# Attention and Fourier mixing on one core: the last head pairs of the first query half go to the output projection through DRAM, two pairs to one set of products

## The chip, the core and the metric

The kernel runs on one core of a Trainium2 chip. Its engines work side by side and wait for each other by semaphores: PE (TensorE, matrix products; its weight loads are listed apart as PEld), ACT (ScalarE), DVE (VectorE), POOL (GpSimd) and SP (SyncE, which here only issues DMAs). Each engine works through its own instructions in the order of the program. A DMA can be issued from SP, from ACT or from POOL, each with a queue of its own; the same 16 DMA engines carry them. The metric is the device time of one execution in microseconds (us); lower is better.

## The reference

Two branches over one input x (2048 rows, 512 columns), mixed by a gate per row:

```python
qkv = (x @ wqkv).reshape(B, S, 3, H, Dh)          # H = 32 heads of Dh = 16
p = softmax(q @ k.T * Dh ** -0.5)                 # per head, 2048 x 2048
a = concat_heads(p @ v) @ wo                      # the output projection
b = dft_seq_re @ (x @ dft_hid_re.T) - dft_seq_im @ (x @ dft_hid_im.T)
g = sigmoid((x * gate_w).sum(-1))
out = g * a + (1 - g) * b
```

Operands of the large products are held as a rounded part and a rest ("hi" and "lo", names ending in h and l); a product is then three: hi·hi, hi·lo, lo·hi.

## The kernel before, in words

The projections, the scans for the softmax's row maxima and most of the Fourier branch come first. The rest is one hand-written loop of 512 steps (line 991), 32 for each of the 16 pairs of heads (16 per half of the queries, h = 0 and 1, of 1024 queries). In a step the scores of one block of 128 keys against 1024 queries go through PE (qk, line 210) and their exponentials through ACT (lines 234 and 242); the products with the values (pv, line 755) are collected in the PSUM bank pvb and run two steps' worth at a time, at even steps. Beside that, each step from 301 on takes one piece of other PE work from the generator `outputs` (`next(fill)`): in an even step before the scores, in an odd step after them, so that two pieces stand together on PE. The pieces are: the last ten row blocks of the Fourier sum (`spectral`, steps 301 to 460), then the output projection: `mix_heads` (pairs 0 to 11), `mix_some` for t = 8, 9, 10, and `mix_some` for t = 0, 1, 2 in steps 505 to 510. The order in which an engine issues its work is the order of the program's text.

**How a pair comes to the projection.** When a pair's half of the queries is summed, `quotients` copies pvb to ob (line 764) and moves the sums of the exponentials into lc by POOL DMAs (767). Some steps later (10; 7 for pair 14; 3 for pair 15) `divide` takes reciprocals (773), spreads them over rb through DRAM (774, 776), multiplies (777) and splits into oh and ol (784, 785). In ob a pair occupies four groups of 32 rows, one for each quarter of the half's queries (c) and each head (j), with 16 rows of values in each: half of the rows carry nothing. Pairs 0 to 13 are written to the DRAM tensors o_d by two POOL DMAs (790). From there they come back without the empty rows: `output_rows` (835) for pairs 0 to 11, four pairs in 128 rows, and `output_rest` (843) for pairs 12 and 13, as 64 rows for each c. Pair 14 (both halves) and pair 15's first half stay in SBUF as they are, rows with gaps; pair 15's second half goes by another way after the loop.

**The products for pairs 12 to 15.** `direct[h]` is the list of their operands for a half, `w4` the list of the rows of wo that belong to them, both of three: k = 0 for pairs 12 and 13 together, k = 1 for pair 14, k = 2 for pair 15. `mix_rest(t, ps, k)` is three products of two matmuls each, one matmul for the row block t and one for t + 4, on 64 rows of the array each. `mix_some(t, parts)` runs k = 0 in one step, all others in the next, and takes the sums into the result on DVE (853); it has parts (0, 1, 2) for t = 0, 1, 2, whose rows are then stored (926), and (0, 1) for t = 8, 9, 10. Block t = 3 and the rest of the second half are finished after the loop by `part`, with `part(3, 0)` in the last step, `part(3, 1)` and `part(3, 2)` placed between the steps of the last pair's division (lines 1051 to 1065).

`output_operands` loads wo's rows for w4 (lines 808 to 816): for k = 0 64 rows twice; for k = 1 and 2 it clears a tile on DVE (810) and loads four groups of 16 rows (812), gaps between.

The lines that the change touches have these numbers: 778 to 788 (where oh and ol are put, and who is not written to DRAM), 809 to 812, 844, 938, 954, 968, 1037 and 1056.

Of the kernel before, what the change touches and what calls it, by code (L numbers as in the profile page):

```python
# [10 lines left out]
F32 = mybir.dt.float32  # L11
F32R = mybir.dt.float32r
# [6 lines left out]
P = 128  # L19
# [3 lines left out]
DH = 16  # L23
NP = H // 2
NB = S // P
ND = D // P
# [27 lines left out]
def build(tc, xT, wqkv, wo, wrT, wiT, cr, ci, gate, out):  # L54
    nc = tc.nc
    with ExitStack() as ctx:
# [130 lines left out]
        def block(i):  # L187
            return big.tile([P, 512], F32R, tag=f"b{i}", name=f"b{i}")
# [541 lines left out]
        with ExitStack() as pa:  # L730
# [40 lines left out]
            def divide(p, h, ob, lc):  # L771

                nc.vector.reciprocal(lc, lc)  # L773
                nc.gpsimd.dma_start(r_d[p][h].rearrange("n (s e) -> (n s) e", e=16), lc)  # L774
                for n, (c, j, r) in enumerate(quads):
                    nc.gpsimd.dma_start(rb[r:r + DH, :], r_d[p][h][n:n + 1, :].to_broadcast([DH, 512]))
                nc.gpsimd.tensor_mul(ob, ob, rb)
                kept = p >= NP - 2
                if p == NP - 2:
                    oh, ol = block(28 + 2 * h), block(29 + 2 * h)  # L780
                else:
                    pool, *tags = (cw, "chi", "clo") if kept else (ap, "oh", "ol")
                    oh, ol = (pool.tile([P, 512], F32R, tag=tag, name=tag) for tag in tags)
                nc.gpsimd.tensor_copy(oh, ob)
                nc.gpsimd.tensor_sub(ol, ob, oh.bitcast(F32))
                if kept:
                    direct.setdefault(h, []).append((oh, ol))
                    return
                for i, s in enumerate((oh, ol)):
                    nc.gpsimd.dma_start(o_d[p // 4][i][h, :, p % 4], s.bitcast(F32))  # L790

# [7 lines left out]
            def output_operands():  # L799

                for n in range(2 * ND - 2):
                    b = [block(6 + 2 * n + i) for i in range(2)]
                    raw = (ap.tile([P, D], F32, tag="craw", name="wor", bufs=2) if n == ND - 2 else
                           ap.tile([P, D], F32, tag="take", name="wor", bufs=3))
                    if n < ND - 1:
                        nc.sync.dma_start(raw, wo[n * P:n * P + P, :].rearrange("(h e) m -> e h m", e=DH))
                    else:
                        base = D - (8, 4, 2)[n - ND + 1] * DH
                        if n >= ND:
                            nc.vector.memset(raw, 0.0)  # L810
                            for c, j, r in quads:
                                nc.sync.dma_start(raw[r:r + DH, :], wo[base + DH * j:base + DH * j + DH, :])
                        else:
                            for r in (0, 64):
                                nc.sync.dma_start(raw[r:r + 64, :],
                                                  wo[base:base + 64, :].rearrange("(h e) m -> e h m", e=DH))
                    raws_.append((raw, b))
                    if n % (ND - 1) == ND - 2:
                        yield
                        yield  # L820
                        for raw, b in raws_:
                            yield
                            nc.vector.tensor_copy(b[0], raw)
                            nc.vector.tensor_sub(b[1], raw, b[0].bitcast(F32))
                            (w2 if n < ND - 1 else w4).append(b)
                        raws_.clear()
                        yield
# [9 lines left out]
            def output_rest(h):  # L837

                a = [block(24 + 2 * h + i) for i in range(2)]
                for i in range(2):  # L840
                    for c in range(2):
                        src = o_d[ND - 1][i][h, c, 0:2].rearrange("p (j r) s -> r (p j) s", j=2)
                        nc.sync.dma_start(a[i][64 * c:64 * c + 64, :].bitcast(F32), src[0:DH])
                direct[h].insert(0, a)

            def load_y(c):
                y4 = stk.tile([P, 4, D], F32, tag="stk", name="y4")
# [80 lines left out]
            def mix_some(t, parts):  # L928

                ps = pair_banks()  # L930
                ps = ps[:, 0, :], ps[:, 1, :]
                for k in parts:
                    mix_rest(t, ps, k, k == parts[0], k == parts[-1])
                    if k == parts[0]:
                        yield
                for j in range(2):
                    take_in(t + 4 * j, ps[j])
                if parts[-1] == 2:
                    store_out(t)
                yield  # L940

            def outputs():

                for t in range(NB - LATER, NB):
                    yield from spectral(t)
                for c in range(NC):
                    for t in range(4 * c, 4 * c + 4):
                        yield from mix_heads(t, (2, 2, 2, 3) if t < 2 * SLOW and t % 2 == 0 else (4, 5))
                    if c < 2:
                        output_rows(c + 2)  # L950
                for t in (8, 9, 10):
                    yield from mix_some(t, (0, 1))
                for t in range(3):
                    yield from mix_some(t, (0, 1, 2))
                yield

            groups = {}
# [1 line left out]
            def part(t, *ks):  # L959

                if t not in groups:
                    if t in (3, 9):
                        ps = pair_banks()
                        groups[t] = ps[:, 0, :], ps[:, 1, :]
                    else:
                        groups[t] = bank2() if t == 8 else (bank(), pvb if t == 11 else bank())
                for k in ks:
                    mix_rest(t, groups[t], k, k == 0 or 7 < t < 11, k == 2)

            now = [0]  # L970
            fill, operands = outputs(), output_operands()
# [19 lines left out]
            for step in range(NP * PERIODS):  # L991
                p, i = step // PERIODS, step % PERIODS
                h, kb = i // NB, i % NB
                now[0] = step
                if i == 18:
                    load_use(p + 1)
                if step in (MIX - 24, MIX - 20):
                    load_unit()
                if step == MIX - 12:
                    split_unit()  # L1000
                if OUT - 10 <= step < OUT - 4 or step >= OUT + 4:
                    next(operands, None)
                if step in (OUT - 12, OUT + 1):
                    output_rows(int(step > OUT))
                if step in (OUT - 25, (NP - 1) * PERIODS):
                    for c in range(2):
                        load_y(c + 2 * (step > OUT))
                if step >= MIX and step % 2 == 0:
                    next(fill)
                if step == 0:  # L1010
                    pend.append((p, h, kb, ahead[:2]))
                    continue
                es = ahead[2:] if step == 1 else [qk2(p, h, kb, 0)]
                if step == 1:
                    es.append(qk2(p, h, kb, 1))
                    flush()
                if late:
                    late.pop(0)()
                if step == 2:
                    es.append(qk2(p, h, kb, 1))  # L1020
                if step > 1:
                    next_scan()
                if step > 2:
                    es.append(qk2(p, h, kb, 1))
                if step >= MIX and step % 2:
                    next(fill)
                if step == NP * PERIODS - 1:
                    part(3, 0)
                done = None
                for _ in range(min(len(pend), 1) if step < MIX else 0 if step % 2 else 2):  # L1030
                    done = flush()
                if done and done[2] == NB - 1:
                    halved.append((step + (10 if done[0] < NP - 2 else 7 if done[0] < NP - 1 else 3), quotients(*done[:2])))
                if halved and halved[0][0] <= step:
                    p_, h_ = halved[0][1][:2]
                    divide(*halved.pop(0)[1])
                    if p_ == NP - 2:
                        output_rest(h_)
                pend.append((p, h, kb, es))
            flush()  # L1040
            flush()
# [11 lines left out]
            turned, spread = bank(), bank()  # L1053
            for q in blocks_:
                nc.tensor.transpose(turned[:, q], ob[:, q], ident)
            part(3, 2)
            rl = sm.tile([P, 16], F32, tag="lc", name="lc")
            nc.vector.reciprocal(rl.rearrange("p (s n) -> p s n", n=4),
                                 turned.rearrange("p (s n m) -> p s n m", n=4, m=32)[:, :, :, DH])
# [56 lines left out]
```

## Time and profile before

| | |
|---|---|
| time, median of 3 runs | 1726.92 us (1726.63 to 1727.53) |
| span of the profiled execution | 1725.2 us |
| what lies around the span (median less span) | 1.7 us |
| instructions | 36082 |
| PE busy | 1713.5 us (99%) |
| ACT, DVE, POOL busy | 1506.8, 1089.1, 648.7 us |
| HBM read, written | 129.63 MB, 61.61 MB |

The span is the time from the first to the last instruction of one execution that the hardware profiler recorded; the profile gives no other time for that execution. Times in the profile's rows are microseconds from the start of the span unless marked ns. L185 is line 185 of the kernel; where a helper issues an operation, the line is the helper's (185 is `halves_of`, which issues all matmuls of `spectral`, `mix_heads` and `mix_rest`). "xy<-b,c" is an operation that writes tile xy from tiles b and c. A row in square brackets ends with the idle time of the engine before it and what ended it. Some records of matmuls can be missing, so a count in a row can be a little low.

### The profile page before, as it was taken

How to read it: one execution, taken by the hardware profiler on the slowest of the kernel's cores; microseconds unless marked ns; L12 is line 12 of the kernel's file. 1: busy time of each engine (PE TensorE's matmuls, PEld its weight loads, DVE VectorE, ACT ScalarE, POOL GpSimd, SP SyncE). 2: the span in 40 equal slices, each digit the busy share in tenths (PEclk: the TensorE clock that was granted, in tenths of full speed). 3: DMA queues.
4: the chain of work that ended last, by engine and by line, in shares of the span. 5: the costliest groups of instructions: out<-in, count | busy, mean ns of one | idle time of the engine just before them, and what ended most of it. 6: DMA issues, size and time to landing. Idle time of an engine off the chain costs nothing.

```text
span 1725.2 us, 36082 instructions
## 1 busy us (share of the span) xinstructions
PE 1713.5 (99%) x13680; PEld 1044.7 (61%) x13680; DVE 1089.1 (63%) x2059; ACT 1506.8 (87%) x2489; POOL 648.7 (38%) x770
## 2 busy tenths in 40 slices
PE   9999999999999999999999999999999999999998
PEld 7888888988888885333333333333455555555554
DVE  6898888999999996666666666666512212122333
ACT  6447889888888888999999999999988888888886
POOL 3672436655555762223233242322322322223222
PEclk9999999999999999999999999999999999999999
DMA  7783557534337663243323342351334244265712
GB/s 257 241 285 75 156 158 211 158 112 115 103 111 211 153 136 72 37 73 58 66 59 67 54 82 44 58 107 37 65 80 94 72 110 91 67 150 139 175 36 101
DMA packets 123710, 193.03 MB, mean 112 GB/s; under 512 B 54112, under 2 KB 56656, under 8 KB 116624
## 3 DMA queue, kind: packets, MB, share of 16 engines
q1 hardware_dynamic: 84464, 170.20, 37.7%
q0 software_dynamic: 38496, 19.47, 5.7%
q8 instruction: 107, 1.75, 0.4%
q10 hardware_dynamic: 576, 1.05, 0.2%
q14 instruction: 67, 0.55, 0.1%
HBM read 129.63 MB, written 61.61 MB: 111 GB/s over the span
## 4 chain that ended last, share of the span: by engine, by line
PE 96%; DVE 2%; DMA 1%; issue 1%; ACT 0%; SPq 0%; DVEq 0%; POOL 0%; ACTq 0%; POOLq 0%
PE pvb L755 29%; PE xy L185 25%; PE s L210 19%; PE s L185 9%; PE s L154 9%; PE s L135 5%; DVE fold L160 1%; DMA q_d<-eh 0%; DMA raws<-wqkv 0%; DMA ks<-kf_d 0%; PE s L554 0%; DVE y L853 0%; ACT fold L158 0%; DVE s L278 0%; DVE b L334 0%
## 5 line engine op out<-in xcount | busy, mean ns | idle before, releaser
L234 ACT ACTIVATE eb<-s 128x1024 f32<-128x1024 f32 x512 | 578.7, 1130 | 65.4 <-PE s L210 65.4
L242 ACT ACTIVATE e<-s 128x512 f32<-128x512 f32 x1022 | 608.9, 709 | 0.4 <-PE s L210 0.4
L137 DVE TENSOR_REDUCE mx<-s 128x2 f32<-128x1024 f32 x364 | 441.4, 1224 | 188.7 <-PE s L135 188.5
L755 PE MATMUL pvb<-eb,va 128*17 128x512 f32 x2052 | 513.0, 597 | 0.0
L755 PE MATMUL pvb<-e,va 128*17 128x512 f32 x2044 | 512.1, 597 | 0.0
L160 DVE CUSTOM_DVE_ANT_0 fold<-s,fold 128x512 f32<-128x512 f32 x660 | 443.9, 690 | 52.7 <-PE s L154 24.4
L158 ACT ACTIVATE fold<-s 128x512 f32<-128x512 f32 x660 | 389.9, 603 | 73.3 <-PE s L154 52.3
L210 PEld LDWEIGHTS s<-qs,ks 50*128 50x128 f32 x2048 | 214.9, 184 | 355.2 <-ACT eb L234 255.1
L210 PE MATMUL s<-qs,ks 50*128 50x512 f32 x2048 | 420.0, 434 | 0.0
L185 PE MATMUL xy<-b,c 64*128 64x512 f32 x2448 | 397.3, 392 | 0.3 <-ACT c L333 0.3
L154 PE MATMUL s<-ks,qs 48*128 48x512 f32 x1320 | 315.3, 405 | 1.6 <-DVE mx L160 1.0
L185 PEld LDWEIGHTS xy<-b,c 64*128 64x128 f32 x2448 | 283.9, 187 | 17.6 <-issue 1.0
L154 PEld LDWEIGHTS s<-ks,qs 48*128 48x128 f32 x1320 | 172.9, 184 | 47.0 <-DVE mx L160 12.5
L774 POOL DMA_DIRECT2D r_d<-lc x31 | 18.1, 583 | 456.4 <-DVE lc L773 456.4
L755 PEld LDWEIGHTS pvb<-eb,va 128*17 128x17 f32 x2052 | 70.5, 96 | 189.9 <-issue 182.7
L135 PE MATMUL s<-ks,qs 48*128 48x512 f32 x728 | 151.6, 394 | 0.7 <-DVE mx L137 0.7
L767 POOL DMA_DIRECT2D lc<-ob x124 | 62.9, 514 | 156.3 <-DVE ob L764 156.1
L185 PE MATMUL xy<-w,b 64*128 64x512 f32 x768 | 115.3, 392 | 0.0
L365 POOL TENSOR_TENSOR c<-craw,c 128x512 fp32r<-128x512 f32 x84 | 109.4, 1302 | 6.7
L185 PE MATMUL s<-b,chi 64*128 64x512 f32 x670 | 105.4, 391 | 0.0
L364 POOL CAST c<-craw 128x512 fp32r<-128x512 f32 x84 | 53.3, 635 | 125.1 <-PE xy L185 120.1
L871 DVE CAST chi<-craw 128x512 fp32r<-128x512 f32 x40 | 19.1, 477 | 111.4 <-PE s L185 99.3
(136 smaller groups left out, 1535.2 us busy)
## 6 DMA issues: line engine op xcount, KB each, us to landing
qs<-q_d SPq DMA_DIRECT2D x66, 256.0 KB
craw<-ci SPq DMA_DIRECT2D x64, 256.0 KB
craw<-cr SPq DMA_DIRECT2D x60, 256.0 KB
ks<-k_d SPq DMA_DIRECT2D x44, 256.0 KB
qs<-q_d SPq DMA_DIRECT2D x66, 128.0 KB
ab_d<-ab SPq DMA_DIRECT2D x32, 256.0 KB
y_d<-y SPq DMA_DIRECT2D x32, 256.0 KB
o_d<-oh POOLq DMA_DIRECT2D x28, 256.0 KB, 13.8
```

Source lines behind the costliest of these rows:

```text
L135: nc.tensor.matmul(ps[:, j, :], qs[b:b + 48, qb * P:(qb + 1) * P], ks[b:b + 48, c * 512:(c + 1) * 512], start=True, stop=True)
L137: nc.vector.tensor_reduce(mx[p][:, :, qb, c], ps, axis=AX.X, op=ALU.max)
L154: nc.tensor.matmul(ps, qs[b:b + 48, qb * P:(qb + 1) * P], ks[b:b + 48, c * 512:(c + 1) * 512], start=True, stop=True)
L158: nc.scalar.activation(fold[j], ps, AF.Relu)
L160: nc.vector.tensor_tensor_reduce(out=fold[j], in0=ps, in1=fold[j], scale=1.0, scalar=-3.0e38, op0=ALU.add, op1=ALU.max, accum_out=mx[p][:, ...
L185: nc.tensor.matmul(ps[j], lhs[r], rhs[r], start=first, stop=last)
L210: nc.tensor.matmul(pss[j], ks[b:b + 50, kb * P:(kb + 1) * P], qs[b:b + 50, q0:q0 + 512], start=True, stop=True)
L234: nc.scalar.activation(e, ps, AF.Exp, scale=SCALE)
L242: nc.scalar.activation(e[j], pss[j], AF.Exp, scale=SCALE)
L365: sub(lo, raw, hi.bitcast(F32))
L755: nc.tensor.matmul(pvb[r:r + VC, :], va[:, kb, 2 * p + j, :], es[c][j], start=kb == 0, stop=kb == NB - 1, tile_position=(0, r))
L767: nc.gpsimd.dma_start(lc[32 * n:32 * n + 32, :], ob[r + DH:r + VC, :].rearrange("p (s e) -> p s e", e=16))
```

## The change

`divide` writes pair 14 (both halves) and the first half of pair 15 to DRAM like the pairs before them. A new function `output_last(h)` reads them back without gaps: for h = 0 pairs 14 and 15, 64 rows for each c; for h = 1 pair 14 alone, 32 rows for each c, with the other 32 cleared on DVE. `output_last(1)` is called with the division of pair 14's second half, `output_last(0)` with the division of pair 15's first half. The weights for k = 1 become the 64 rows of wo for pairs 14 and 15 together, so in the first half of the queries `mix_rest(t, ps, 1)` covers both pairs and k = 2 is left out there. In the second half k = 2 is still pair 15, with gaps.

```diff
                 nc.gpsimd.tensor_mul(ob, ob, rb)
-                kept = p >= NP - 2
-                if p == NP - 2:
-                    oh, ol = block(28 + 2 * h), block(29 + 2 * h)
-                else:
-                    pool, *tags = (cw, "chi", "clo") if kept else (ap, "oh", "ol")
-                    oh, ol = (pool.tile([P, 512], F32R, tag=tag, name=tag) for tag in tags)
+                oh, ol = (ap.tile([P, 512], F32R, tag=tag, name=tag) for tag in ("oh", "ol"))
                 nc.gpsimd.tensor_copy(oh, ob)
                 nc.gpsimd.tensor_sub(ol, ob, oh.bitcast(F32))
-                if kept:
-                    direct.setdefault(h, []).append((oh, ol))
-                    return
                 for i, s in enumerate((oh, ol)):
                     nc.gpsimd.dma_start(o_d[p // 4][i][h, :, p % 4], s.bitcast(F32))
...
-                        if n >= ND:
+                        if n == ND:
+                            for r in (0, 64):
+                                nc.sync.dma_start(raw[r:r + 64, :], wo[base:base + 64, :])
+                        elif n > ND:
                             nc.vector.memset(raw, 0.0)
...
-                direct[h].insert(0, a)
+                direct[h] = [a]
+
+            def output_last(h):
+
+                a, n = [block(28 + 2 * h + i) for i in range(2)], 2 - h
+                for i in range(2):
+                    for c in range(2):
+                        src = o_d[ND - 1][i][h, c, 2:2 + n].rearrange("p (j r) s -> (p j) r s", j=2)
+                        nc.sync.dma_start(a[i][64 * c:64 * c + 32 * n, :].bitcast(F32), src[:, 0:DH])
+                        if n == 1:
+                            nc.vector.memset(a[i][64 * c + 32:64 * c + 64, :].bitcast(F32), 0.0)
+                direct[h].append(a)
...
-                if parts[-1] == 2:
+                if t < NB // 4:
                     store_out(t)
...
-                    yield from mix_some(t, (0, 1, 2))
+                    yield from mix_some(t, (0, 1))
...
-                    mix_rest(t, groups[t], k, k == 0 or 7 < t < 11, k == 2)
+                    mix_rest(t, groups[t], k, k == 0 or 7 < t < 11, k == (2 if t > 3 else 1))
...
                     if p_ == NP - 2:
                         output_rest(h_)
+                    if p_ == NP - 2 + (h_ == 0):
+                        output_last(h_)
...
-            part(3, 2)
```

## The prediction

> **What bounds the kernel now.** I read the page's busy times first, then its chain of work that ended last, then the same chain in order of time for the last 75 us, where all of the change's products stand.
>
> ```profile
> PE 1713.5 (99%) x13680; PEld 1044.7 (61%) x13680; DVE 1089.1 (63%) x2059; ACT 1506.8 (87%) x2489; POOL 648.7 (38%) x770
> ...
> PE 96%; DVE 2%; DMA 1%; issue 1%; ACT 0%; SPq 0%; DVEq 0%; POOL 0%; ACTq 0%; POOLq 0%
> ```
>
> ```profile
> 1679.43 1.41 PE s L185 x11
> ...
> 1683.79 1.38 PE s L185 x12
> ...
> 1688.17 1.41 PE s L185 x12
> ...
> 1692.55 2.09 PE s L185 x16
> 1694.64 0.47 PE s L210 x4
> 1695.11 1.84 PE pvb L755 x16
> 1696.95 0.67 PE s L210 x4
> 1697.62 2.10 PE s L185 x18
> ...
> 1702.69 2.10 PE s L185 x17
> ...
> 1710.65 0.89 PE s L185 x6
> ```
>
> The columns are start, duration and what the chain did. PE holds the chain nearly throughout, so here PE work that goes is time that goes. Two steps make one round: a group of projection products (L185), scores (L210), values (L755), scores. The groups at 1679.43, 1683.79 and 1688.17 are t = 8, 9, 10 with 12 matmuls, those at 1692.55, 1697.62 and 1702.69 are t = 0, 1, 2 with 18 (16 and 17 where records are missing). A round with 12 takes 1688.17 - 1683.79 = 4.38 us, one with 18 takes 1697.62 - 1692.55 = 5.07. So six matmuls cost 0.69 us, or 0.23 for a product of two, and nothing else takes their place as the bound when they are absent: the rounds of 12 already run in this very loop.
>
> **What is removed from PE.** Six matmuls in each of three rounds: 3 x 0.69 = 2.07 us, and `part(3, 2)` behind the loop.
>
> ```profile
> 1712.06 0.73 PE L185 MATMUL s<-b,chi 64*128 64x512 f32 x4
> 1712.63 0.40 PE L185 MATMUL s<-b,clo 64*128 64x512 f32 x2
> ...
> 1713.00 0.53 PEld L1065 LDWEIGHTS s<-ident,rb 128*128 128x128 f32 x4 [0.41 <-DVE rb L1062]
> ...
> 1712.52 0.76 DVE L1062 TENSOR_TENSOR rb<-s,lc 128x256 f32<-128x256 f32 x2
> ```
>
> That group fills PE from 1712.06 to 1713.03. The transposes behind it (L1065) start at 1713.00 and are put down to DVE's product rb, whose first half of two starts at 1712.52 and so ends near 1712.9. Without the group PE stands idle there instead: gain 0 (at most 0.1 us). ACT's scaling of block 3 can come a little earlier, but what ends last runs through the products of t = 8 to 11 behind these transposes. So the gain is 2.07 us, if the operands are there.
>
> **What is added: a trip through DRAM, and whether it is in time.** There are three trips. The critical one is pair 15's first half, whose division ends last.
>
> ```profile
> 1685.73 0.61 POOL L784 CAST chi<-ob 128x512 fp32r<-128x512 f32 x1
> 1686.42 1.27 POOL L785 TENSOR_TENSOR clo<-ob,chi 128x512 fp32r<-128x512 f32 x1
> ...
> 1585.89 1.28 POOL L785 TENSOR_TENSOR ol<-ob,oh 128x512 fp32r<-128x512 f32 x1
> 1587.12 0.88 POOL L790 DMA_DIRECT2D o_d<-oh  x1
> 1587.99 0.82 POOL L790 DMA_DIRECT2D o_d<-ol  x1
> ```
>
> ```profile
> o_d<-oh POOLq DMA_DIRECT2D x28, 256.0 KB, 13.8
> o_d<-ol POOLq DMA_DIRECT2D x28, 256.0 KB, 13.9
> rb<-r_d POOLq DMA_DIRECT2D x124, 32.0 KB, 2.0
> ```
>
> ```profile
> DMA to landing us min/median/max: 9.4/9.8/10.1
> ...
> DMA to landing us min/median/max: 9.1/13.9/20.2
> ```
>
> In the run before, both parts are ready in SBUF at 1686.42 + 1.27 = 1687.69, five us ahead of their use. After the change the two stores follow: pair 13's, in the rows of 1585 to 1588, start 1.23 and 2.10 us after the subtraction's start, so here at 1687.65 and 1688.52. How long they take is the decisive term. Over all 56 stores of this line, issue to landing took 9.1 to 20.2 us, median 13.9. The first of the two landing rows is a pair of stores issued at 818 us while no other bulk transfer ran: 9.4 for oh, 10.1 for ol. From 1687 on the DMA engines are idle too (one instruction fetch of 16 KB in the nine us from 1686 on):
>
> ```profile
> q8 instruction: 1, 0.02, 0.7%
> ...
> L843 SPq DMA_DIRECT2D b<-o_d x8: 514/545/1276, 1613.4 to 1640.2; - x8
> ```
>
> So I take the quiet pair, which is the nearest row: oh lands at 1697.05, ol at 1698.6. SP waits for each and then issues two loads of 128 KB, 0.55 us each (the 514/545/1276 row, ns). A quiet transfer of 32 KB takes 2.0 us to land; the second load, issued 0.6 later, is then there 2.6 us after the store (bounds 2 and 4). So the hi operand is ready at 1699.65, the lo operand at 1701.2.
>
> Needed: t = 0's k = 1, at the head of step 506, comes 0.69 us after the group's start, at 1692.55 + 0.69 = 1693.24. Nothing before that point is shortened. PE waits there, and behind it in PE's own order stand the scores of step 506, so ACT, which has only finished step 505's exponentials, waits too, then the values, then DVE. Nothing covers this: about 6.4 us idle until the hi products (four matmuls, 0.46 us), again until 1701.2, and the last product ends at 1701.45. Before, the whole group of 18 ended at 1694.64: **+6.8 us** at this place. The other two rounds then give 2 x 0.69 = 1.39 back: +5.4.
>
> **The clock after the stall.** The granted TensorE clock is 1.00 in all of the loop. After the last matmul, at 1718.1, it stays and then falls:
>
> ```profile
> 1718.00:1721.00 3.00, 0.07 (x2) 0.00 (x0) 2.16 (x4) 0.02 (x1) 2.03 (x2) 1.00 1.03 379
> 1721.00:1724.00 3.00, 0.00 (x0) 0.00 (x0) 0.00 (x0) 0.00 (x0) 0.00 (x0) 0.52 0.86 319
> ...
> 2.30:3.30 1.00, 1.00 (x6) 1.00 (x5) 1.00 0.96 238
> ...
> 4.30:5.30 1.00, 0.85 (x8) 0.61 (x6) 1.00 0.87 303
> ```
>
> The first two rows (the sixth value behind the colon-separated stretch and its length is the clock) show that some 3 us of idle PE are enough: 0.52 in the stretch from 1721. An idle of 6.4 us is longer than that. How long it then stays at half is bounded by the program's start: there the warm-up transposes go from 6 per us to 8 per us within 3 to 4 us of work. PE-bound work at half clock loses half of that time; part of it falls into the wait for lo. I take **+1.5 us**, bounds 0 (no fall) and 3.4.
>
> The Trainium skill (TensorE: Matmul & The Clock Gate, Part 1: The HAM clock gate) says the clock is halved after an idle window of about 3.4 us and comes back after about 3.4 us of sustained work, with windows that run free of the program. The trace agrees for the fall (about 3 us); by the rule alone the loss would be an estimated 1.7 us.
>
> **The other trips are in time.** Pair 14's second half:
>
> ```profile
> 1655.69 1.29 POOL L785 TENSOR_TENSOR b<-ob,b 128x512 fp32r<-128x512 f32 x1
> ...
> 1647.53 0.24 DVE L773 RECIPROCAL lc<-lc 128x16 f32<-128x16 f32 x1
> 1651.15 1.54 DVE L853 SCALAR_TENSOR_TENSOR y<-s,g,y 128x512 f32<-128x512 f32 x2 [3.38 <-PE s L185]
> 1596.25 1.03 DVE L810 MEMSET wor<- 128x512 f32 x2
> ```
>
> Stores at 1656.9 and 1657.8, landed by 1668, loaded by 1671; needed at 1679.43 + 0.69 = 1680.1. Even the slowest landing (20.2) brings it to 1680.6. Its first half is divided 33 us earlier and needed only with pair 15's. The four clears of 32 rows cost at most 0.52 each (half of the 1.03 row), 2.1 us of DVE right behind the reciprocal of 1647.53, in an idle stretch of 3.38: cost 0; if they had no cover, 2.1. One clear and two of eight small loads of wo go, on DVE and SP beside a bound PE: 0. On SP, only the stores of finished rows stand behind `output_last`, and they come after the products anyway. On POOL nothing stands behind the last two stores before 1713. The tiles oh and ol, now used by three more divisions, are read out (1668) long before the next one writes them (1685.73).
>
> **Sum.** +6.8 - 1.39 + 1.5 + 0 = +6.9 on the span: 1725.2 + 6.9 = 1732.1. The runs' median lies 1.7 over the span: **1733.8 us**.
>
> **Rivals.**
> *The store is quick, no stall.* SP's stores of finished rows are of the same size:
>
> ```profile
> 1705.61 0.99 SPq L926 DMA_DIRECT2D out_dram<-y  x2
> ...
> GB/s 0 0 0 0 0 0 0 0 0 0 0 0 191 328 410 300 355 410 382 382 382 410 383 328 382 437 355 410 410 355 301 82 0 0 0 0 0 0 0 0
> ```
>
> Two of 256 KB, the first issued at 1705.61, and the traffic (slices of 0.075 us from 1705.5) is over at 1707.9: 2.3 us. At that rate ol is in DRAM at 1690.9 and loaded at 1693.5, just before lo's turn at 1693.24 + 0.46; the change then gives its 2.07 us whole: 1724.85, not slower. It decides if both parts are back by 1693.7. Against it: no store of this line landed in under 9.1 us, quiet or not. 5%.
> The Trainium skill (DMA: Bandwidth & Descriptors, Anatomy of one DMA — SWDGE) has about 2.0 us plus the bytes at 436 GB/s for a DMA issued from GpSimd, an estimated 2.6 us for these 256 KB; by that the stall would all but vanish. The rows of this very store (9.4 where quiet) do not agree.
>
> *Stall, but the clock holds* (two short idles instead of one): 1733.8 - 1.5 = 1732.3. For it: the hi products break the idle. 12%.
>
> *The store takes its median*, 13.9 instead of 10.1: +3.8, 1737.6. For it: half of all stores did; against it, those ran beside other traffic, these do not. 10%.
>
> *SP is held earlier.* If `output_rest(0)` had to wait for pair 14's store (same DRAM tensor, other rows; stored from about 1623), the loads behind it on SP, `output_rows(2)` and the rows of y for the second half, would come at 1642 to 1648 rather than by 1640, where t = 8 needs them near 1639: about +5 more, 1739. Against it: SP loads the next rows of y_d 0.38 us after the start of a store to others of its rows, without waiting:
>
> ```profile
> 1550.92 0.33 SPq L893 DMA_DIRECT2D y_d<-y  x1
> 1551.30 0.44 SPq L879 DMA_DIRECT2D y<-y_d  x1
> ```
>
> 3%.
>
> **Chances and range.** The forecast has 70%. Its own bounds: a store 2 us quicker than the quiet pair and no clock loss gives 1730.3, a store 2 us slower and 3 us of loss 1737.3. With the median store inside, the range is 1730.8 to 1738.5; outside it are the quick store, the held SP and tails. A difference of 0.2% (3.45 us) is about what a measurement of this kernel tells from none; even the quick store would gain only 2.07, so it counts as the same. Faster 0.02, same 0.07 (with the lower tail), slower 0.91.
>
> **What would show it.** In the changed kernel's trace: a first group of t = 0 cut in two with an idle PE of some 6 us ended by the DMA from o_d; two stores near 1687.7 with 9 to 10 us to landing; a clock under 1.00 in the us after it; rounds of 4.38 for t = 1 and 2 once the clock is back; no new wait around 1639 or 1680. The prediction is wrong if the stores land within 5 us, or if PE's idle ends by anything else than that load.

## The result: slower, and by nearly twice what was forecast

| | before | after |
|---|---|---|
| time, median | 1727.03 us (1726.63 to 1727.53, 5 runs) | 1739.8 us (1739.1 to 1741.2, 5 runs) |
| ratio to before, 95% interval | | 1.0076 [1.0065, 1.0087] |
| span of the profiled execution | 1725.2 us | 1737.3 us (its own time: 1739.1) |

The forecast was 1733.8 with a range to 1738.5. The spans differ by 12.1 us where 6.9 were forecast, the medians by 12.8.

The busy times and the chain of waits by engine, on the page of the changed kernel:

```profile
PE 1714.9 (99%) x13656; PEld 1037.3 (60%) x13656; DVE 1088.6 (63%) x2062; ACT 1506.7 (87%) x2489; POOL 653.5 (38%) x776
...
PE 94%; DMA 2%; DVE 1%; issue 1%; ACT 0%; POOL 0%; SPq 0%; DVEq 0%; POOLq 0%; ACTq 0%
```

24 matmuls are gone, as intended (13680 to 13656), yet PE's busy time grew by 1.4 us, and 2% of the chain, which was 1% before, are now DMAs. The matmuls of line 185 in order of time, in the timeline of the changed kernel's PE (start, duration, what, and in brackets the idle time before it with what ended it):

```profile
1687.93 1.57 PE L185 MATMUL s<-b,b 64*128 64x512 f32 x12
1692.31 0.87 PE L185 MATMUL s<-b,b 64*128 64x512 f32 x6
1701.12 0.79 PE L185 MATMUL s<-b,b 64*128 64x512 f32 x1 [7.94 <-DMA b<-o_d]
1702.40 1.22 PE L185 MATMUL s<-b,b 64*128 64x512 f32 x3 [0.49 <-DMA b<-o_d]
1704.01 0.79 PE L185 MATMUL s<-b,b 64*128 64x512 f32 x1 [0.40 <-DMA b<-o_d]
1705.30 0.79 PE L185 MATMUL s<-b,b 64*128 64x512 f32 x1 [0.49 <-DMA b<-o_d]
1710.61 1.55 PE L185 MATMUL s<-b,b 64*128 64x512 f32 x12
1714.99 1.54 PE L185 MATMUL s<-b,b 64*128 64x512 f32 x12
```

Up to t = 0's k = 0 at 1692.31 nothing has moved (1692.39 before). Then come four waits for the operands from DRAM, one for each of the four loads, and each matmul after a wait takes 0.79 us where 0.39 is usual: the clock. The groups of t = 1 and 2 stand 4.38 us apart, as forecast. The chain in order of time shows of what the waits are made (start, duration, what the chain did):

```profile
1686.43 1.27 POOL ol L780
...
1688.52 11.43 DMA o_d<-ol
...
1699.97 0.51 SPq L847
...
1700.53 4.72 DMA b<-o_d
...
1705.30 0.79 PE s L185
1706.09 0.85 PE s L210 x3
1706.95 3.16 PE pvb L755 x16
...
1712.16 0.49 PE s L210 x4
1712.64 1.84 PE pvb L755 x16
```

The store of ol takes 11.43 us, its two loads from the first issue to the last matmul's start 1705.30 - 1699.97 = 5.3. (The chain follows the load that was issued last; by e4 below the wait would have been about as long with a quicker store of ol.) Behind them the scores and values take 0.85 + 3.16 where the next round takes 0.49 + 1.84. The last projection matmul of t = 0 ends at 1706.09; before, it ended at 1694.64. The granted clock by stretches of 4 us (behind each stretch stand its length, the busy time of PE, PEld, DVE, ACT and POOL, then the clock, the share of the DMA engines and GB/s):

```profile
1692.00:1696.00 4.00, 1.18 (x10) 0.60 (x8) 0.00 (x0) 2.00 (x3) 0.00 (x0) 0.99 0.23 66
1696.00:1700.00 4.00, 0.00 (x0) 0.00 (x0) 0.00 (x0) 0.00 (x0) 0.00 (x0) 0.50 0.15 52
1700.00:1704.00 4.00, 2.01 (x4) 0.78 (x4) 0.00 (x0) 0.00 (x0) 0.00 (x0) 0.50 0.25 94
1704.00:1708.00 4.00, 3.49 (x14) 1.44 (x18) 1.41 (x2) 1.44 (x3) 0.00 (x0) 0.50 0.10 38
1708.00:1712.00 4.00, 4.00 (x29) 1.80 (x23) 0.00 (x0) 1.98 (x5) 0.00 (x0) 0.80 0.29 109
```

It is at half from 1696, some 3 us after the last matmul, until after 1708. The mean of 0.80 in the last stretch means half speed up to about 1709.6, some 4 us after dense work set in at 1705.30. The single matmuls between the four waits had not brought it back: from 1700 to 1704 PE was busy for 2.01 of 4 us, at 0.50.

The Trainium skill (TensorE: Matmul & The Clock Gate, Part 1: The HAM clock gate) asks for about 3.4 us of sustained work, in windows that run free of the program, before the clock returns; the 4 us here agree with that.

**What the loads look like.** During the loads of four heads the 16 DMA engines are about a quarter busy, and the rate is steady. In the DMA view of the changed kernel, 40 slices of a stretch from 1700 to 1704 us, loads of four heads, and one from 1667 to 1674, `output_last(1)` with its loads of two heads:

```profile
GB/s 102 123 102 82 102 123 102 82 102 102 123 82 102 102 102 61 82 62 61 102 102 41 61 41 102 102 82 102 123 102 82 102 123 82 102 82 143 82 82 102
...
GB/s 0 0 35 0 0 0 35 35 47 70 47 47 47 47 59 59 47 47 47 47 59 59 47 23 47 70 47 47 47 47 59 59 47 47 47 35 0 0 0 0
DMA packets 136, 0.26 MB, mean 37 GB/s; under 512 B 8, under 2 KB 8, under 8 KB 136
```

Four heads: about 94 GB/s. Two heads: 47, half of it. The four loads of the second stretch have 8 packets under 512 B beside their 128 rows, two for each load. So the rate goes with the count of the outermost dimension in the transfer's access pattern, some 23.5 GB/s for each of it. `output_rest` reads the same kind of rows with the 16 rows of a head outermost; `output_last` has the heads outermost. That became theory A.

The Trainium skill (DMA: Bandwidth & Descriptors, Why a DMA increments its semaphore by 16 and not by 1) says that a transfer runs on the largest number of DMA engines up to 16 that divides the outermost dimension of both its sides, and that each of them ends with a write to the semaphore. The rates of 94 and 47 and the two small packets for each load of two heads agree with 4 and 2 engines.

### The profile page after: what moved, and what is told of

It is laid out like the page before. It is cut to its first block, busy times and chain, and to the rows that moved or that the text cites. A ratio compares the mean times of both kernels' runs of the same rounds, so it can differ in the third digit from the quotient of the medians.

```text
span 1737.3 us, 36050 instructions
## 1 busy us (share of the span) xinstructions
PE 1714.9 (99%) x13656; PEld 1037.3 (60%) x13656; DVE 1088.6 (63%) x2062; ACT 1506.7 (87%) x2489; POOL 653.5 (38%) x776
## 4 chain that ended last, share of the span: by engine, by line
PE 94%; DMA 2%; DVE 1%; issue 1%; ACT 0%; POOL 0%; SPq 0%; DVEq 0%; POOLq 0%; ACTq 0%
PE pvb L755 28%; PE xy L185 25%; PE s L210 18%; PE s L154 9%; PE s L185 9%; PE s L135 5%; DVE fold L160 1%; DMA o_d<-ol 1%; DMA q_d<-eh 0%; DMA raws<-wqkv 0%; DMA raws<-xT 0%; DMA b<-o_d 0%; ACT fold L158 0%; PE s L554 0%; DVE y L859 0%
## 5 line engine op out<-in xcount | busy, mean ns | idle before, releaser
L154 PE MATMUL s<-ks,qs 48*128 48x512 f32 x1320 | 315.1, 404 | 1.6 <-DVE mx L160 1.0
L135 PE MATMUL s<-ks,qs 48*128 48x512 f32 x728 | 146.6, 394 | 0.7 <-DVE mx L137 0.7
L859 DVE SCALAR_TENSOR_TENSOR y<-s,g,y 128x512 f32<-128x512 f32 x49 | 35.9, 749 | 86.6 <-PE s L185 86.1
```

The source lines that it names most:

```text
L135: nc.tensor.matmul(ps[:, j, :], qs[b:b + 48, qb * P:(qb + 1) * P], ks[b:b + 48, c * 512:(c + 1) * 512], start=True, stop=True)
L154: nc.tensor.matmul(ps, qs[b:b + 48, qb * P:(qb + 1) * P], ks[b:b + 48, c * 512:(c + 1) * 512], start=True, stop=True)
```

## The experiments

The kernel before, timed on the same chip, took 1726.89 us beside e1 to e4, 1726.69 beside e5 to e8 and 1726.63 beside e9.

| run | what | median us | ratio to before, 95% |
|---|---|---|---|
| e1_rmajor | loads with 16 rows outermost | 1735.72 | 1.0050 [1.0036, 1.0064] |
| e2_sp_store | pair 15's stores from SP | 1738.56 | 1.0068 [1.0056, 1.0081] |
| e3_both | e1 and e2 | 1736.28 | 1.0052 [1.0040, 1.0065] |
| e4_warm | changed kernel, PE kept at work in the wait | 1736.86 | 1.0057 [1.0045, 1.0070] |
| e5_pool_split | e1, stores cut by c, from POOL | 1728.94 | 1.0012 [1.0003, 1.0020] |
| e6_sp_split | e1, stores cut by c, from SP | 1725.82 | 0.9997 [0.9988, 1.0006] |
| e7_direct | no DRAM: copies SBUF to SBUF | 1725.80 | 0.9995 [0.9986, 1.0003] |
| e8_left_out | before, less the matmuls of k = 2 | 1724.61 | 0.9988 [0.9979, 0.9997] |
| e9_two_queues | e7, copies on two queues | 1725.64 | 0.9994 [0.9985, 1.0003] |

### The shape of the loads

```diff
...
                     for c in range(2):
-                        src = o_d[ND - 1][i][h, c, 2:2 + n].rearrange("p (j r) s -> (p j) r s", j=2)
-                        nc.sync.dma_start(a[i][64 * c:64 * c + 32 * n, :].bitcast(F32), src[:, 0:DH])
+                        src = o_d[ND - 1][i][h, c, 2:4].rearrange("p (j r) s -> r (p j) s", j=2)
+                        nc.sync.dma_start(a[i][64 * c:64 * c + 64, :].bitcast(F32), src[0:DH])
...
```

The rows of wo for k = 1 are loaded in the same order, and zeros written to DRAM at the start take the place of the clears in SBUF.

> The changed kernel with the read-back in the order of output_rest: the 16 rows of a head outermost instead of the four heads (weights in the same order; pair 15's slot of the second half is zeroed once in DRAM instead of the clears in SBUF). The stores are unchanged. Theory A (the transfer is carried by as many DMA engines as its outermost dimension has, four here): each of the four loads runs on 16 engines, the lo operand is there 2.6 us after its store's landing instead of 5.3, and the time falls from 1739.8 by 2.7 to about 1737. Theory B (the loads are slow because they run behind the tail of the store): the order changes nothing, 1739 to 1740.

1735.72 us: 4.1 under the changed kernel (the intervals of the two ratios, [1.0036, 1.0064] and [1.0065, 1.0087], just miss each other, so the size is rough). The chain of e1 in order of time:

```profile
1687.14 9.94 DMA o_d<-oh
1697.08 0.02 issue
1697.09 2.67 DMA b<-o_d
1699.76 0.04 issue
1699.81 2.66 PE s L185 x6
1702.47 0.85 PE s L210 x4
1703.32 3.32 PE pvb L759 x16
```

The first load of hi is there 2.67 us after oh's landing, where it took 4.0 in the changed kernel (1697.1 to 1701.12), and the six matmuls now run without a wait between them (at half clock, 2.66 us). The edit gave more than the 2.7 expected, in part by chance: ol's store landed earlier here, 1698.3 beside 1699.95, and it did so in e4 too (1697.9), where the loads are those of the changed kernel. Theory B falls for the changed kernel: the time fell with the order of the loads, and in e4 the earlier landing alone brings the last operand no sooner. It does not fall everywhere, as e3 shows below.

### Who issues the stores

```diff
+                    queue = nc.sync if p == NP - 1 else nc.gpsimd
-                    nc.gpsimd.dma_start(o_d[p // 4][i][h, :, p % 4], s.bitcast(F32))
+                    queue.dma_start(o_d[p // 4][i][h, :, p % 4], s.bitcast(F32))
```

> The changed kernel with the two stores of pair 15's first half issued from SP instead of POOL; the loads stay in their order of four heads outermost. Theory A (the stall is the sum of a slow store from POOL, 9.5 and 11.4 us, and a slow load, 5.3 us): the stores land in about 2.4 us, oh near 1688.8 and ol near 1690.2, the loads 5.3 later, 1694.1 and 1695.5 on the clock of the changed kernel; a stall of 1 to 2 us is left, too short for the clock to fall, and the two other rounds give 1.4 back: about 1726.7. Rival: the stores are slow because of what they write (128 rows to DRAM), not because of who issues them: 1739 to 1740.

> Both edits of the two runs before together: stores of pair 15's first half from SP, read-back with 16 rows outermost. Theory A: oh and ol are in DRAM near 1688.8 and 1690.2, back by 1691.4 and 1692.8, before their turns at 1693.2 and 1693.6; no stall, the clock holds, and the gain of 18 matmuls is left whole: 1727.0 less 2.07, 1725.0. Rival (the removed matmuls were not worth 0.69 us a group, or the group taken out behind the loop was): 1727.0 or under 1724.5.

1738.56 and 1736.28 us: both expectations of theory A are missed by 11 to 12 us, and e3 is no better than e1. SP's timeline in e2, and the DMA traffic from 1687 to 1694 there:

```profile
1686.10 0.51 SPq L783 DMA_DIRECT2D o_d<-oh  x1
1687.47 0.51 SPq L783 DMA_DIRECT2D o_d<-ol  x1
1694.05 6.20 SPq L848 DMA_DIRECT2D b<-o_d  x4
```

```profile
GB/s 0 35 35 12 12 47 47 0 47 47 0 0 47 47 0 47 47 47 140 35 47 47 59 59 47 47 47 47 59 59 47 47 47 59 59 47 47 47 47 59
DMA packets 141, 0.30 MB, mean 43 GB/s; under 512 B 2, under 2 KB 2, under 8 KB 140
```

The first load waits until 1694.05: oh's store took 7.9 us from SP too, at 47 GB/s again, and ol's stands behind it at the same rate. So the store can be slow for the loads' reason: its pattern is [2, 64, 512], the two quarters c outermost. That is theory A2. That the slow store is POOL's doing, which I had assumed, falls here: from SP it is 1.5 us quicker and still takes 7.9.

In e3 the loads have the quick order, and yet the first operand comes 5.5 us after its load was issued, as SP's and PE's timelines show:

```profile
1694.33 6.29 SPq L853 DMA_DIRECT2D b<-o_d  x4
...
1699.79 1.52 PE L185 MATMUL s<-b,b 64*128 64x512 f32 x4 [6.43 <-DMA b<-o_d]
```

In the DMA view of e3 from 1694 to 1701 the traffic rises to 316 GB/s with the loads, is back at 47 from about 1697.3 until ol's store has landed (1699.4), and ends near 1699.7. So here, where store and loads come from the same queue, the loads seem to have waited for the tail of the store, as theory B had it; no run tests that by itself.

### The clock

```diff
+                for _ in range(16 if t == 0 else 0):
+                    mix_rest(t, ps, 0, True, True)
                 for k in parts:
                     mix_rest(t, ps, k, k == parts[0], k == parts[-1])
```

> The changed kernel with PE kept at work in the wait: the six matmuls of t = 0, k = 0 are run 16 times more before their real turn (11 us, their sums are overwritten). Nothing in the operands' way is changed. Theory A (the clock falls to half in the wait and costs about 2.3 us after it): the operands come at the same moment, the clock stays at 1.00, and the time falls by about 2.3 to 1737.5. Rival (the clock costs nothing, the work behind the wait is held by something else): 1739 to 1740.

1736.86 us, 2.9 under the changed kernel. The intervals of the two ratios, [1.0045, 1.0070] and [1.0065, 1.0087], overlap at their ends, so the size is rough, the place is not. The chain of e4 in order of time:

```profile
1698.45 0.50 SPq L847
...
1699.00 6.20 DMA b<-o_d
...
1705.24 0.50 PE s L185
1705.74 0.47 PE s L210 x3
1706.21 1.84 PE pvb L755 x16
1708.06 0.66 PE s L210 x4
```

The last operand comes at the same time as in the changed kernel, 1705.24 beside 1705.30. What follows takes 0.50 + 0.47 + 1.84 = 2.81 us, there 0.79 + 0.85 + 3.16 = 4.80: 2.0 us are the clock's, at this place alone.

This run shows one thing more. Its store of ol landed after 9.9 us and not 11.43, and the last load was issued at 1699.00 and not at 1700.53, but the last operand came no sooner. From the landing of oh, 1697.2 here and 1697.1 there, it is 8.1 and 8.2 us in the two kernels. The four loads, 0.52 MB, take 5.6 us at the 94 GB/s above (an estimate); I take the rest to be the first one's issue and landing. So PE waited for four loads, one behind the other from oh's landing on, and when ol landed hardly counted.

### The shape of the stores

```diff
                 for i, s in enumerate((oh, ol)):
-                    nc.gpsimd.dma_start(o_d[p // 4][i][h, :, p % 4], s.bitcast(F32))
+                    if p == NP - 1:
+                        for c in range(2):
+                            nc.gpsimd.dma_start(o_d[p // 4][i][h, c, p % 4], s[64 * c:64 * c + 64, :].bitcast(F32))
+                    else:
+                        nc.gpsimd.dma_start(o_d[p // 4][i][h, :, p % 4], s.bitcast(F32))
```

Both kernels also have the loads of e1; the second issues these stores from SP.

> The changed kernel with the read-back of 16 rows outermost, and each store of pair 15's first half cut into two by c, 64 rows of 2 KB each, still issued from POOL. Theory A2 (a transfer of outermost dimension 2, as this store has, is carried by two DMA engines at some 47 GB/s in all, whoever issues it; POOL has no part in it): four stores with 64 rows outermost run on 16 engines, the last is issued near 1690 and lands some 2.5 us later, 1692.5; loaded by 1695.1 (turn of lo: 1693.6): 1.5 us of stall, clock at 1.00, the two other rounds give 1.4 back: about 1727. Rival (stores from POOL are slow because POOL writes their descriptors): landing still 9 us after issue, time 1735 to 1736, as with the uncut store.

> The same as the run before it, with the four stores issued from SP. Theory A2: oh is on its way at 1686.4 and landed by 1689.0, ol by 1690.4; back by 1691.6 and 1693.0, before their turns at 1693.2 and 1693.6. No stall, no fall of the clock, the gain of the removed matmuls whole: 1727.0 less 2.07, about 1725. Rival (a store to DRAM and the read of it cost over 7 us in sum whatever their shape): a stall of some us, 1729 or more.

From POOL, 1728.94 us; the row of the four stores' landing, of their line in e5:

```profile
DMA to landing us min/median/max: 2.3/2.5/4.3
```

Cut in two, three of the four land in a quarter of the time. The rival (POOL's own work on descriptors) falls. The time is 1.9 us over the expectation: the last of the four took 4.3, and why is not shown. From SP, 1725.82: about 0.9 under the kernel before, which is within the noise (its interval holds 1), and 0.8 over the expectation. PE's timeline in e6:

```profile
1692.44 1.63 PE L185 MATMUL s<-b,b 64*128 64x512 f32 x11
1694.41 0.50 PE L185 MATMUL s<-b,b 64*128 64x512 f32 x1 [0.34 <-DMA b<-o_d]
1697.71 1.54 PE L185 MATMUL s<-b,b 64*128 64x512 f32 x12
```

The wait has shrunk from about 12 us to parts of one. The next group stands 5.27 us behind, where 4.38 would be without any.

### No trip through DRAM

```diff
+                if p >= NP - 2:
+                    if p == NP - 2:
+                        lasts[h] = [block(28 + 2 * h + i) for i in range(2)]
+                    for i, s in enumerate((oh, ol)):
+                        for c, j, r in quads:
+                            at = 64 * c + 32 * (p - NP + 2) + 16 * j
+                            (nc.sync if p == NP - 1 else nc.gpsimd).dma_start(
+                                lasts[h][i][at:at + DH, :].bitcast(F32), s[r:r + DH, :].bitcast(F32))
+                    return
...
```

`output_last` issues no loads any more. In e9 the queue is SP only where `p == NP - 1 and (i == 0 or c == 0)`.

> The changed kernel without the trip through DRAM for pairs 14 and 15: the 16 rows of each head are copied from oh and ol into the compact operands by one DMA each, SBUF to SBUF (pair 15 from SP, eight DMAs; pair 14 from POOL). One landing of about 2 us in place of two. Theory A2: hi is there at about 1690.5, lo at about 1692.3, before their turns: about 1725, as with the cut stores from SP, with more room. Rival (DMAs of 16 rows are slow too): a stall, 1729 or more.

> The kernel of the direct copies, with the four copies of pair 15's ol shared between SP (two) and POOL (two). There, eight copies from SP took 0.6 us each and the last one's data came at 1693.7 on its clock, which held the lo products by some 0.5 us. If the issue on one queue is what was left of the stall, lo is there about 1 us earlier, the wait is gone and the time is that of the kernel with the matmuls simply left out: 2.1 us under the kernel before, about 1724.7 beside 1726.8. If not, it stays about 1 us under.

1725.80 and 1725.64 us: 0.9 and 1.0 under the kernel before. In e9's chain in order of time the group of t = 0 is

```profile
1688.78 1.41 PE s L185 x12
...
1693.16 1.71 PE s L185 x9
...
1697.85 1.38 PE s L185 x12
```

0.3 us longer than the group before it; in e7 it was 1.98. The two queues took half of that wait away, but the medians do not tell the two kernels apart, and the expectation of 1724.7 was missed by 0.9. Neither interval is clear of 1: no version that does all of the work is shown to be faster than the kernel before.

### The gain alone

```diff
...
-                    yield from mix_some(t, (0, 1, 2))
+                    yield from mix_some(t, (0, 1))
...
-            part(3, 2)
```

> The kernel before with the matmuls of k = 2 left out for t = 0 to 3 and nothing in their place: pair 15 is missing from the first half of the queries. No trip through DRAM. It measures the gain of the removed matmuls alone. Prediction's value: three groups of 0.69 us in the loop and nothing behind it: 1727.0 less 2.07, 1725.0. Rival (the group behind the loop was worth its 0.9 us too): 1724.0.

1724.61 us, 2.08 under 1726.69; ratio 0.9988 [0.9979, 0.9997]. That is 3 x 0.69, with nothing for the group behind the loop, but the interval (0.5 to 3.6 us) holds the rival's 3.0 too. The chains of the two kernels in order of time settle it, the kernel before first:

```profile
1711.55 0.59 PE s L1055 x4
1712.13 0.90 PE s L185 x6
1713.03 0.74 PE s L1065 x4
```

```profile
1709.33 0.60 PE s L1055 x4
...
1710.79 0.77 PE s L1064 x4
```

From one set of transposes to the other it is 1.48 us with the group between them and 1.46 without. So the group is worth nothing, and some 2.1 us are the most that a quicker way for these operands could gain here.

## Why the prediction fell short

**Right.** The place and its cause: PE waits at t = 0's k = 1 for the trip of pair 15's first half, and nothing covers it. The removed matmuls are worth 0.69 us a group (rounds of 4.38), and the group behind the loop nothing (e8). oh's store: 9.4 taken, landed at 1697.12 after 9.47. The clock falls after some 3 us. Pair 14's second half is in time. SP was not held earlier: `output_rest(0)` issued at 1612.8 (1613.4 before).

**Wrong in size, two terms**, both in one direction:

| term of the sum | predicted | measured |
|---|---|---|
| oh's landing to the last operand (the rest of ol's store, then its loads) | 1697.05 to 1701.2: 4.15 us | 1697.12 to 1705.30: 8.2 us, +4.0 |
| half clock | 1.5 us | 2.0 in e4's rows after the wait, 2.9 in its median: +0.5 to +1.4 |

Together +4.5 to +5.4 on 6.9, against 12.1 measured.

**The step that failed** is the load's price. The prediction put it as "A quiet transfer of 32 KB takes 2.0 us to land; the second load, issued 0.6 later, is then there 2.6 us after the store (bounds 2 and 4)". Measured were 5.35 us from ol's landing to the last operand, outside these bounds. The row it was priced from is of a quarter of a load's size and has the 16 rows of a head outermost, and so has the row of `output_rest` from which the issue time came. The diff shows the new loads in another order, "(p j) r s", and I did not ask what the order changes: they ran at 94 GB/s, so that lo's loads stood behind hi's, and it took 8.2 us from oh's landing to bring all four. In the order of e1 the first load is there after 2.67 us and no matmul of the group waits again.

ol's own store took 11.43 us where 10.1 was taken. By e4, where it took 9.9 and the last operand came no sooner, that is not what made the wait longer.

**The rival of a quick store** was priced from a good row (SP's stores of finished rows, 2.3 us) and for a wrong reason. It compared queues, SP and POOL, where the two stores also differ in shape: 128 rows outermost there, two quarters here. e2 took the queue and kept the shape, and the store stayed slow; e5 kept the queue and cut the store to 64 rows outermost, and it landed in 2.3 to 2.6 us but for one of 4.3. The Trainium skill (DMA: Bandwidth & Descriptors, Anatomy of one DMA — SWDGE) has the figure that I weighed there; for the 128 KB of each of e5's stores it gives an estimated 2.3 us. Three of them agree with it, and the uncut store, for which it gives 2.6, does not (9.5 and 11.4).

**The clock** was under-sized because I let part of the half clock pass in the wait for lo; the four loads came one by one, PE stayed idle for half of that time, and the clock came back only near 1709.6. The rows of the program's start, by which I bounded how long it stays at half, have a granted clock of 1.00 throughout, so they show nothing of a half clock.

## What to carry to other kernels

Price a new DMA by a row of the same shape, above all of the same outermost dimension on both sides, and not by its bytes or its queue: 2 outermost ran at 47 GB/s here, 4 at 94, and the same rows with 16 or 64 outermost landed in 2.3 to 2.7 us, but for one store of 4.3 (e5) and the loads of e3 behind a slow store from their own queue. Count the loads that are issued just before it as well. A trip through DRAM that was long hidden elsewhere in a kernel says nothing of what it costs near the end, where its reader is three steps behind its writer. When PE bounds a kernel and waits over 3 us, add the half clock behind the wait, and count its end from where dense work begins again: here that was some 4 us.

## What I had not expected of the hardware

A store issued from SP was nearly as slow as from POOL when its outermost dimension was 2 (7.9 us for oh in e2, about 9.5 from POOL). Cut in two it became quick from both: from POOL 2.3 to 2.6 us but for one, and from SP, in e6, the first load of what was stored could be issued 2.6 us after the store. All 28 pairs of these stores in the kernel before run in that shape, 9 to 20 us each, hidden. The half clock outlasted the wait by some 4 us (1705.30 to 1709.6): PE's work between the loads, 2.01 us in the 4 from 1700, had not ended it.
